# One string of single-engine steps for attention, seams and FFN, with accumulating transfers for part of the third factors

## The chip, the cores and the metric

The kernel runs on one core of a Trainium2 chip. Its engines are TensorE (PE, matrix products into PSUM), VectorE (DVE), ScalarE (ACT), GpSimd (POOL) and SyncE (SP, which here issues transfers); each works through its own queue in order, and they wait for each other through semaphores. The metric is the time of one execution on the device in microseconds (us). Most executions of one kernel agree within 0.3%.

## What is computed

The reference is an attention block with learned inducing points, followed by a gated feed-forward network (FFN) on every token. Four batches of 12416 tokens with 128 channels, 32 inducing vectors, an FFN width of 1536:

```python
def mab(q, kv):
    s = scale * (q @ kv.transpose(0, 2, 1))
    s = s - s.max(-1, keepdims=True)
    a = np.exp(s)
    a /= a.sum(-1, keepdims=True) + 1e-09
    return a @ kv
h = mab(I, x)                       # (4, 32, 128)
x = mab(x, h)                       # (4, 12416, 128)
rms = np.sqrt(np.mean(x * x, axis=-1, keepdims=True) + 1e-06)
xn = x / rms * rms_g
g = xn @ w_gate
silu = g * (1.0 / (1.0 + np.exp(-g)))
val = xn @ w_val
return (silu * val @ w_out)
```

## The kernel before

**Blocks.** A batch is cut into 25 units of 512, 480 or 256 tokens, and the FFN width into 12 columns of 128. A block (b, u, j) is batch, unit and column; there are 1200. For each, `slot` issues the gate product (L743), the silu on ACT (L751), the value product (L754) and the product of silu and value on DVE (L760), which is the factor u of the block. Gate and value products are in float32r, one step of the PE array per column; the attention output is carried as an upper and a lower half, so that these products have both halves in one contraction.

**The output product, in two ways.** For 381 blocks, "plain", the factor goes through one float32 product with `wo` (L676), which the PE array takes in four steps. For the other 819 it is split into an upper and a lower part, and three float32r products take the place of one float32 product: upper part by upper weights and lower part by lower weights into a PSUM bank `u` (L700, L702), and the third, a combination of both parts by a combination of both weights, into `acc` (L676). The combination of the parts is called the third factor below. It is made in `three`:

- kind "sums" (619 blocks): the factor stays in its PSUM bank (the product L760 writes `gv` over itself), ACT makes the upper part (L725), DVE the lower from the upper part in SBUF and the factor in PSUM (L726);
- kind "differences" (200 blocks): the factor is written to an SBUF tile `u`, ACT makes the upper part (L729), POOL the lower (L730), ACT scales the upper (L734);
- in both, one slot later, POOL makes the third factor from both parts with a two-input instruction into a tile of its own (L735).

A set of three tiles (upper, lower, third) is taken from four sets in `xn` buffers and two lent from the `sg` and `sv` weight buffers while they are free; this is why L735 and L726 appear in the profile with the tiles `xn`, `sg` and `sv`.

**Order.** `slots` runs over blocks. Within a slot, the string `ordered` says at which points how many output products of either kind go to PE; `banks` says which of the five PSUM banks each product gets, `holders` which SBUF tile a factor gets; `places` says in which slot each step of the attention of the next batch and each step of a seam stands. A seam (`seam`) turns attention weights into the next unit's normalised operand: transposes and products on DVE, a product on PE (L523), a power on POOL (L539), a multiplication on POOL (L543), a lower half on POOL (L556). Steps may hold instructions of several engines (a score product and its DVE transpose, for instance). The first 47 us, before the first gate product, are written out by hand in `first`.

**Transfers.** All are issued by SP, except three on ACT's queue; POOL issues none.

Of the kernel before, what the change touches and what calls it, by code (L numbers as in the profile page):

```python
# [18 lines left out]
P = 128  # L19
R = 4  # L20
# [3 lines left out]
def kernel(  # L24
# [75 lines left out]
    RING, RESERVE, HELD, SILU = 4, 7, 9, 3  # L100
    LENT = (RING, RING + 1)
# [41 lines left out]
    def load_channels(b, s, k):  # L143

        w = R * per[s]
        if not k:
            xT[b, s] = xtp.tile([P, w * m], F32, name=f"xT{s}")
        nc.sync.dma_start(out=xT[b, s][ts(k, m), :].rearrange("p (w c) -> p w c", c=m),
                          in_=xrows[ds(b * N + start[s], P * per[s]), ts(k, m)].rearrange("(i w) c -> i w c", i=m))
# [159 lines left out]
    def attention(b, load_next):  # L309
# [34 lines left out]
        def scores1(s):  # L344
            nc.vector.tensor_scalar(out=sc[b][:, cols1[s]], in0=scores(s, indT[:], R, per[s]), scalar1=1.0, scalar2=None,
                                    op0=ALU.mult, op1=ALU.max, accum_out=st["gmx"][:, s:s + 1])
# [31 lines left out]
        def sum_h(*sets):  # L378
# [12 lines left out]
            if b and sets[0]:  # L391
                nc.vector.tensor_tensor(out=hl[:, 0:C], in0=hl[:, 0:C], in1=ps[:, 0:C], op=ALU.add)
            elif b:
                nc.scalar.copy(out=hl[:, 0:C], in_=ps[:, 0:C])

        def fold_l():

            nc.vector.reduce_sum(out=st["hl"][:, C:C + 1], in_=st["ls"][:, 0:st["n"]], axis=AX.X)
            ps = bank()
            nc.tensor.matmul(ps[:, 0:1], fold[:].rearrange("p q m -> p (q m)"), st["hl"][:, C:C + 1], start=True, stop=True)  # L400
            rl = st["rl"] = small.tile([P, 1], F32, name="rl")
            nc.vector.reciprocal(out=rl[:], in_=ps[:, 0:1])
# [8 lines left out]
        def turn_h():  # L411

            ps = bank()
            nc.tensor.matmul(ps[:, 0:P], st["hn"], fold[:].rearrange("p q m -> p (q m)"), start=True, stop=True)
            hT = st["hT"] = once.tile([P, P], F32, name="hT")
            if b:
                nc.scalar.copy(out=hT[:], in_=ps[:, 0:P])
                hg = st["hg"] = once.tile([P, P], F32, name="hg")
                nc.scalar.activation(hg[:], ps[:, 0:P], AF.Copy, scale=gam)
            else:  # L420
                nc.vector.tensor_copy(out=hT[:], in_=ps[:, 0:P])
# [5 lines left out]
        def square_h():  # L427
# [4 lines left out]
            ps = bank()  # L432
            nc.tensor.matmul(ps[:, 0:m], st["hT"][:], st["hT"][:, 0:m], start=True, stop=True)
            for q in range(R):
                to, of_ = gram[b][ts(q, m), ts(q, m)], ps[ts(q, m), 0:m]
                nc.scalar.activation(to, of_, AF.Copy, bias=1e-6, scale=1.0 / C)

        def scores2(s):
            ps = scores(s, st["hT"][:, 0:m], quarters[s], per2[s])
            nc.vector.transpose(out=sc[b][rows2[s], cols2[s]], in_=ps)  # L440

        def row_max(s):
            mx = st["mx2"] = small.tile([P, 16], F32, name="mx2")[rows2[s], 0:per2[s]]
            nc.vector.reduce_max(out=mx, in_=weights(b, s), axis=AX.X)

        def sub_max(s):
            n, v, mx = per2[s], weights(b, s), st["mx2"]
# [16 lines left out]
        def stack(i):  # L464


            ps = bank()
            for c, w in enumerate(st.pop(("w", i))):
                nc.tensor.matmul(ps[ts(c, m), :], st["hg"][:, 0:m], w, start=True, stop=True)
            hi, lo = st["halves", i] = [worker([P, 512], F32R, n) for n in ("whi", "wlo")]  # L470
            rows = slice(0, NC * m)
            nc.scalar.copy(out=hi[rows, :], in_=ps[rows, :])
            nc.vector.tensor_tensor(out=lo[rows, :], in0=ps[rows, :], in1=hi[rows, :].bitcast(F32), op=ALU.subtract)
# [33 lines left out]
    def seam(b, s):  # L507
# [41 lines left out]
        def split():  # L549
# [4 lines left out]
            else:  # L554
                nc.vector.tensor_copy(out=hi[rows, 0:w], in_=aT[rows, 0:w])
            engine.tensor_tensor(out=lo[rows, 0:w], in0=aT[rows, 0:w], in1=hi[rows, 0:w].bitcast(F32), op=ALU.subtract)  # L556

        return [turn_a, square, times, scale, root, apply, turn_b, split]
# [11 lines left out]
    plain, kara, waiting = [], [], []  # L570

    def soon(k, step):

        waiting.append([k, step])

    def wait():

        for one in waiting:
            one[0] -= 1
        while any(not one[0] for one in waiting):  # L580
            one = next(one for one in waiting if not one[0])
            waiting.remove(one)
            one[1]()

    def give(group):

        for kind in group:
            (plain if kind == "p" else kara).pop(0)()

    def split_wo(step):  # L590

        if not step:
            kws["first"] = xnp.tile([P, half + NK, C], F32R, name=f"xn{full - 1}")
            rings = [xnp.tile([P, RING, 512], F32R, name=f"xn{full - 4 + n}") for n in range(3)]
            kws["sets"] = [[ring[:, n, :] for ring in rings] for n in range(RING)]
            idle.extend(range(RING))
# [10 lines left out]
        for g in range(2):  # L607
# [8 lines left out]
            if at == 4:  # L616
                nc.gpsimd.tensor_tensor(out=part(2, g)[0], in0=part(1, g)[1], in1=part(0, g)[1], op=ALU.subtract)
            if at == 6:
                scaled(0, g, 4096.0)

    idle, leaving = [], []

    def lend(b, k, idle, leaving):

        if k == (20 if not b else 2):
            idle += LENT
            return True
        if b + 1 < B and k == 184:
            leaving += [n for n in LENT if n not in idle]
            idle[:] = [n for n in idle if n not in LENT]  # L630
        assert k != 192 or not leaving

    def give_back(n, idle, leaving):

        leaving.remove(n) if n in leaving else idle.append(n)

    def lend_tiles():

        tiles = [stk.tile([P, F], F32R, name=name) for name in ("sg", "sv")]
        kws["sets"][RING:] = [[t[:, ts(n, 512)] for n in range(3)] for t in tiles]  # L640

    def split_last(step):

        n = NJ - NK
        if not step:
            kws["last"] = xtp.tile([P, 3 * n, C], F32R, name="xT0")
        one, (whi, wlo, ws) = wo[:, NK:NJ, :], (kws["last"][:, ts(kind, n), :] for kind in range(3))
        if step == 0:
            nc.scalar.activation(whi, one, AF.Copy, scale=1.0 - 2.0 ** -13)
            nc.gpsimd.tensor_tensor(out=wlo, in0=one, in1=whi.bitcast(F32), op=ALU.subtract)  # L650
        if step == 1:
            nc.scalar.activation(wlo, wlo.bitcast(F32), AF.Copy, scale=4096.0)
            nc.gpsimd.tensor_tensor(out=ws, in0=wlo.bitcast(F32), in1=whi.bitcast(F32), op=ALU.subtract)
        if step == 2:
            nc.scalar.activation(whi, whi.bitcast(F32), AF.Copy, scale=4096.0)

    def weight_of(kind, j):
        if j >= NK:
            return kws["last"][:, kind * (NJ - NK) + j - NK, :]
# [3 lines left out]
    def ffn(b, u):  # L663

        s, q = units[u]
        T = per2[s] * m
        a = moving.pop((b, u))
        sg, sv = stacks[b]
        acc = ps_acc.tile([P, 512], F32, name="acc")
        nk = sum((b, u, j) in kinds for j in range(NJ))  # L670
        st = {"left": NJ, "k": nk}
        if nk:
            st["o"] = None

        def project(lhsT, rhs, to):
            nc.tensor.matmul(to, lhsT, rhs, start=st["left"] == NJ, stop=st["left"] == 1)  # L676
            st["left"] -= 1
            if not st["left"]:
                soon(1, finish)

        def finish():
            o = st["o"] if nk else outp.tile([P, 512], F32, name="o")
            whole = o[:, 0:T].rearrange("p (q n) -> p q n", q=R)
            if nk:
                nc.vector.tensor_tensor(out=whole, in0=in_order(acc[:, 0:T]), in1=whole, op=ALU.add)
            else:
                nc.vector.tensor_copy(out=whole, in_=in_order(acc[:, 0:T]))

            def turn():
                nc.vector.transpose(out=o[:, 0:T], in_=o[:, 0:T])  # L690
                soon(2, lambda: store(o))

            soon(1, turn)

        def project3(j, where):
            if st["k"] == nk:
                st["u"] = ps_u.tile([P, 512], F32, name="u3")
            ups = st["u"]
            hi, lo, d = (one[:, 0:T] for one in kws["sets"][where])
            nc.tensor.matmul(ups[:, 0:T], weight_of(0, j), halves_in_turn(hi), start=st["k"] == nk, stop=False)  # L700
            st["k"] -= 1
            nc.tensor.matmul(ups[:, 0:T], weight_of(1, j), halves_in_turn(lo), start=False, stop=not st["k"])  # L702
            if not st["k"]:
                o = st["o"] = outp.tile([P, 512], F32, name="o")
                nc.scalar.activation(o[:, 0:T].rearrange("p (q n) -> p q n", q=R), in_order(ups[:, 0:T]), AF.Copy,  # L705
                                     scale=1.0 + 2.0 ** -12)
# [609 lines left out]
```

## Time and profile before

| what | value |
|---|---|
| time, three runs | 1538.06 us median (1537.92 to 1538.15) |
| profiled execution | 1538.19 us, span 1536.4 us |
| PE | 1518.3 us busy, 99% of the span |
| DVE | 1442.3 us, 94% |
| POOL | 1418.5 us, 92% |
| ACT | 1292.2 us, 84% |
| transfers by SP | 36.2% of 16 DMA engines' span |
| granted PE clock | 1.0 in every slice |

The profile's span is the time from the first to the last instruction of one profiled execution; 1.8 us of the measured time lie outside it. Busy shares are the union of an engine's instructions. A matmul is shown with a length of about 380 ns, but the next begins about 213 ns later, so a PE that is "busy" may still have small waits in it. A group line gives the source line, engine, operation, tiles, shapes and count, then the busy time in us and the mean length in ns, then the idle time before it and what ended that. In the timeline the columns are start in us, length in us, engine, line, operation and tiles.

### The profile page before, as it was taken

How to read it: one execution, taken by the hardware profiler on the slowest of the kernel's cores; microseconds unless marked ns; L12 is line 12 of the kernel's file. 1: busy time of each engine (PE TensorE's matmuls, PEld its weight loads, DVE VectorE, ACT ScalarE, POOL GpSimd, SP SyncE). 2: the span in 40 equal slices, each digit the busy share in tenths (PEclk: the TensorE clock that was granted, in tenths of full speed). 3: DMA queues.
4: the chain of work that ended last, by engine and by line, in shares of the span. 5: the costliest groups of instructions: out<-in, count | busy, mean ns of one | idle time of the engine just before them, and what ended most of it. 6: DMA issues, size and time to landing. Idle time of an engine off the chain costs nothing.

```text
span 1536.4 us, 26105 instructions
## 1 busy us (share of the span) xinstructions
PE 1518.3 (99%) x7141; PEld 1091.8 (71%) x7141; DVE 1442.3 (94%) x2519; ACT 1292.2 (84%) x2501; POOL 1418.5 (92%) x1158
## 2 busy tenths in 40 slices
PE   8999999999999999999999999999999999999998
PEld 6556667767776667776777667676677777777776
DVE  6999999999999998999999999899999999999997
ACT  5777889888888889887988888978798888888886
POOL 1379999999999999999999999899989999999997
PEclk9999999999999999999999999999999999999999
DMA  7345535435453242634444323353222222122221
GB/s 282 91 81 94 97 60 114 90 78 91 67 92 69 38 93 37 137 84 86 72 78 82 56 59 77 74 120 75 49 39 39 38 36 37 34 40 38 40 40 28
DMA packets 389331, 112.58 MB, mean 73 GB/s; under 512 B 365088, under 2 KB 369728, under 8 KB 386624
## 3 DMA queue, kind: packets, MB, share of 16 engines
q1 hardware_dynamic: 388592, 110.83, 36.2%
q8 instruction: 57, 0.93, 0.3%
q14 instruction: 90, 0.74, 0.2%
q10 hardware_dynamic: 592, 0.08, 0.0%
HBM read 53.95 MB, written 27.00 MB: 53 GB/s over the span
## 4 chain that ended last, share of the span: by engine, by line
PE 90%; DVE 3%; POOL 3%; ACT 2%; issue 1%; DMA 0%; DVEq 0%; POOLq 0%; ACTq 0%
PE acc L676 30%; PE gv L743 17%; PE gv L754 16%; PE u L700 10%; PE u L702 10%; PE gv L341 3%; PE gv L523 1%; PE gv L390 1%; POOL xn L735 1%; ACT silu L751 1%; PE gv L820 1%; DVE u L760 1%; POOL xn L730 0%; DVE gv L760 0%; DMA xn<-in_x_dram 0%
## 5 line engine op out<-in xcount | busy, mean ns | idle before, releaser
L735 POOL TENSOR_TENSOR xn<-xn,xn 128x512 fp32r<-128x512 f32 (+2 forms) x626 | 767.6, 1248 | 34.1 <-DVE xn L726 11.6
L751 ACT ACTIVATE silu<-gv 128x512 f32<-128x512 f32 (+2 forms) x1186 | 683.4, 588 | 98.4 <-PE gv L743 88.1
L754 PE MATMUL gv<-a,sv 128*128 128x512 f32 (+2 forms) x1188 | 551.2, 465 | 1.0 <-ACT silu L751 0.4
L743 PE MATMUL gv<-a,sg 128*128 128x512 f32 (+2 forms) x1188 | 472.2, 398 | 1.6 <-ACT silu L751 0.6
L760 DVE TENSOR_TENSOR gv<-silu,gv 128x512 f32<-128x512 f32 (+2 forms) x616 | 410.6, 673 | 23.4 <-PE gv L754 7.5
L760 DVE TENSOR_TENSOR u<-silu,gv 128x512 f32<-128x512 f32 (+2 forms) x570 | 369.4, 655 | 24.4 <-ACT silu L751 8.8
L676 PE MATMUL acc<-u,wo 128*128 128x512 f32 (+2 forms) x762 | 371.2, 577 | 0.0
L725 ACT ACTIVATE xn<-gv 128x512 fp32r<-128x512 f32 (+2 forms) x472 | 278.1, 589 | 62.3 <-DVE gv L760 47.2
L726 DVE SCALAR_TENSOR_TENSOR xn<-xn,gv 128x512 fp32r<-128x512 f32 (+2 forms) x472 | 312.5, 662 | 13.1 <-ACT xn L725 7.4
L743 PEld LDWEIGHTS gv<-a,sg 128*128 128x128 f32 x1188 | 224.1, 189 | 137.4 <-issue 26.7
L754 PEld LDWEIGHTS gv<-a,sv 128*128 128x128 f32 x1188 | 224.3, 189 | 116.5 <-ACT silu L751 34.4
L700 PE MATMUL u<-xn,xn 128*128 128x512 f32 (+2 forms) x599 | 233.7, 390 | 0.0
L676 PE MATMUL acc<-xn,more 128*128 128x512 f32 (+2 forms) x599 | 225.7, 377 | 1.4 <-POOL xn L735 1.2
L730 POOL TENSOR_TENSOR xn<-u,xn 128x512 fp32r<-128x512 f32 (+2 forms) x154 | 191.0, 1240 | 5.1 <-ACT xn L729 4.7
L676 PEld LDWEIGHTS acc<-u,wo 128*128 128x128 f32 x762 | 142.9, 190 | 32.2 <-issue 15.4
L700 PEld LDWEIGHTS u<-xn,xn 128*128 128x128 f32 x599 | 113.3, 189 | 25.6 <-ACT o L705 8.0
L676 PEld LDWEIGHTS acc<-xn,more 128*128 128x128 f32 x599 | 113.1, 189 | 24.4 <-POOL xn L735 10.2
L735 POOL TENSOR_TENSOR sg<-sg 128x512 fp32r<-128x512 f32 (+2 forms) x97 | 123.4, 1272 | 3.6 <-DVE sg L726 1.0
L735 POOL TENSOR_TENSOR sv<-sv 128x512 fp32r<-128x512 f32 (+1 forms) x96 | 122.1, 1272 | 1.6 <-DVE xT L324 0.2
L702 PE MATMUL u<-xn,more 128*128 128x512 f32 (+2 forms) x304 | 113.0, 372 | 0.0
L702 PE MATMUL u<-xn,xn 128*128 128x512 f32 (+2 forms) x295 | 109.8, 372 | 0.0
L729 ACT ACTIVATE xn<-u 128x512 fp32r<-128x512 f32 (+2 forms) x154 | 95.3, 619 | 14.2 <-DVE u L760 9.2
(229 smaller groups left out, 1894.7 us busy)
## 6 DMA issues: line engine op xcount, KB each, us to landing
out_dram<-o SPq DMA_DIRECT2D x320, 64.0 KB, 2.0
xT<-in_x_dram SPq DMA_DIRECT2D x60, 256.0 KB, 3.9
xn<-in_x_dram SPq DMA_DIRECT2D x60, 256.0 KB, 5.0
a<-hi SPq DMA_DIRECT2D x156, 64.0 KB, 2.0
a<-lo SPq DMA_DIRECT2D x156, 64.0 KB, 2.0
xn<-in_x_dram SPq DMA_DIRECT2D x5, 1024.0 KB, 9.7
xn<-w SPq DMA_DIRECT2D x18, 256.0 KB, 3.0
out_dram<-o SPq DMA_DIRECT2D x64, 60.0 KB, 2.0
```

The costliest lines, as they stand in the source:

```text
L676: nc.tensor.matmul(to, lhsT, rhs, start=st["left"] == NJ, stop=st["left"] == 1)
L700: nc.tensor.matmul(ups[:, 0:T], weight_of(0, j), halves_in_turn(hi), start=st["k"] == nk, stop=False)
L702: nc.tensor.matmul(ups[:, 0:T], weight_of(1, j), halves_in_turn(lo), start=False, stop=not st["k"])
L725: nc.scalar.activation(hi, v, AF.Copy, scale=(1.0 - 2.0 ** -13) * 2.0 ** -12)
L726: nc.vector.scalar_tensor_tensor(out=lo, in0=hi.bitcast(F32), scalar=-4096.0, in1=v, op0=ALU.mult, op1=ALU.add)
L729: nc.scalar.activation(d, v, AF.Copy, scale=1.0 - 2.0 ** -13)
L730: nc.gpsimd.tensor_tensor(out=lo, in0=v, in1=d.bitcast(F32), op=ALU.subtract)
L735: nc.gpsimd.tensor_tensor(out=d, in0=hi.bitcast(F32), in1=lo.bitcast(F32), op=ALU.subtract)
L743: nc.tensor.matmul(g[:, 0:T], sg[:, ts(j, P)], halves_in_turn(a[:, 0:T]), start=True, stop=True)
L751: nc.scalar.activation(sl[:, 0:T], g[:, 0:T], AF.Silu)
L754: nc.tensor.matmul(v[:, 0:T], sv[:, ts(j, P)], halves_in_turn(a[:, 0:T]), start=True, stop=True)
L760: nc.vector.tensor_tensor(out=t[:, 0:T], in0=sl[:, 0:T], in1=v[:, 0:T], op=ALU.mult)
```

## The change

Everything after the first 26 blocks is issued from one string, `program`, of 10,709 letters, each one instruction (or one pair) on one engine; a dot stands for an attention or seam step, listed in `taken`, and those steps are cut so that each has instructions of one engine. `slot`, `three`, `soon`, `wait`, `give` and the lending of weight tiles go away. New letter strings give the banks, workers and tiles. The numbers of gate, value and factor products stay.

Blocks now have seven kinds. P is plain (352 blocks with the first 26). S, T and D are split: S with the factor in PSUM (S and s, 328 blocks), T with the factor in an SBUF tile but the lower part still on DVE (T and t, 307 blocks), D with the factor in SBUF and the lower part on POOL (D and d, 213 blocks). The third factor is written over the lower part, after PE has read it: for a capital letter by POOL's two-input instruction (450 blocks), for a small letter by a transfer that POOL issues and that adds the upper part to the lower part in SBUF (398 blocks). The tiles for factors and parts come from one ring of 19. The core of the diff:

```diff
-        def three(j, t):
-            where = idle.pop(0)
-            hi, lo, d = (one[:, 0:T] for one in kws["sets"][where])
-            v, kind = t[:, 0:T], kinds[b, u, j]
-            if kind == "sums":
-                nc.scalar.activation(hi, v, AF.Copy, scale=(1.0 - 2.0 ** -13) * 2.0 ** -12)
-                nc.vector.scalar_tensor_tensor(out=lo, in0=hi.bitcast(F32), scalar=-4096.0, in1=v,
-                                               op0=ALU.mult, op1=ALU.add)
-            else:
-                nc.scalar.activation(d, v, AF.Copy, scale=1.0 - 2.0 ** -13)
-                nc.gpsimd.tensor_tensor(out=lo, in0=v, in1=d.bitcast(F32), op=ALU.subtract)
-            def rest():
-                if kind != "sums":
-                    nc.scalar.activation(hi, d.bitcast(F32), AF.Copy, scale=2.0 ** -12)
-                nc.gpsimd.tensor_tensor(out=d, in0=hi.bitcast(F32), in1=lo.bitcast(F32), op=ALU.subtract)
-                kara.append(lambda: project3(j, where))
...
+    def times_value():
+        n, b, u, j = next_of("m")
...
+        if kind in "Ss":
+            factor_of[n] = {"u": v[:, 0:T]}
+        else:
+            factor_of[n] = {"u": factor()[:, 0:T]}
...
+    def high():
...
+        hi = t["hi"] = room()[:, 0:T]
+        t["lo"] = room()[:, 0:T]
+        if kind in "Dd":
+            nc.scalar.activation(hi, t["u"], AF.Copy, scale=1.0 - 2.0 ** -13)
+        else:
+            nc.scalar.activation(hi, t["u"], AF.Copy, scale=-(1.0 - 2.0 ** -13) * 2.0 ** -12)
...
+    def low():
+        nc.vector.scalar_tensor_tensor(out=t["lo"], in0=t["hi"].bitcast(F32), scalar=4096.0, in1=t["u"],
+                                       op0=ALU.mult, op1=ALU.add)
+    def low_of_u():
+        nc.gpsimd.tensor_tensor(out=t["lo"], in0=t["u"], in1=t["hi"].bitcast(F32), op=ALU.subtract)
+    def high_down():
+        nc.scalar.activation(t["hi"], t["hi"].bitcast(F32), AF.Copy, scale=-(2.0 ** -12))
+    def project_two():
...
+        nc.tensor.matmul(ups, weight_of(0, j), halves_in_turn(t["hi"]), start=not one["q"], stop=False)
+        nc.tensor.matmul(ups, weight_of(1, j), halves_in_turn(t["lo"]), start=False, stop=last)
+        lists["D" if kinds[n].islower() else "d"].append(n)
...
+    def add_in_place():
+        nc.gpsimd.tensor_tensor(out=t["lo"], in0=t["hi"].bitcast(F32), in1=t["lo"].bitcast(F32), op=ALU.add)
+    def add_by_transfer():
+        nc.gpsimd.dma_start(out=t["lo"].bitcast(F32), in_=t["hi"].bitcast(F32), accum_op=ALU.add)
+    def project_third(name):
+        n = lists[name].pop(0)
+        project(n, weight_of(2, blocks[n][2]), halves_in_turn(factor_of[n]["lo"]), False)
...
-    for b in range(B):
-        unit, at = {}, placed(b)
-        for k, (u, j) in slots(b):
-            groups = picks.pop(0)
...
+    do = {"g": gate, "s": silu, "y": lambda: silu(True), "x": gate_times, "v": value, "m": times_value, "h": high, "l": low,
+          "n": low_of_u, "e": high_down, "q": project_two, "d": add_in_place, "D": add_by_transfer,
+          "r": lambda: project_third("r"), "R": lambda: project_third("R"), "p": project_plain, "E": take_upper, "F": finish,
+          "T": turn_out, "O": store, "a": lambda: gather(*next(gathered))}
+    for name in "".join(program.split()):
+        if name == ".":
+            step, args = micros[int(next(taken))]
+            step(*args)
+        else:
+            do[name]()
```

## The prediction

> **What bounds the kernel now.** First the page's busy shares, then the windows (columns: PE, PEld, DVE, ACT, POOL busy us and counts, PE clock, DMA share, GB/s):
>
> ```profile
> PE 1518.3 (99%) x7141; PEld 1091.8 (71%) x7141; DVE 1442.3 (94%) x2519; ACT 1292.2 (84%) x2501; POOL 1418.5 (92%) x1158
> ```
>
> ```profile
> 400.00:600.00 200.00, 199.57 (x855) 144.13 (x854) 192.79 (x343) 172.25 (x341) 194.91 (x160) 1.00 0.37 67
> 1200.00:1400.00 200.00, 199.07 (x800) 147.09 (x798) 193.61 (x320) 173.08 (x329) 195.71 (x153) 1.00 0.20 37
> ```
>
> PE sets the pace, but DVE and POOL stand at 96 to 98% in these stretches: there is room in none of the three. PE's true work is a little less than its busy share. In the chain two plain products take 1.72 us, so one takes 0.86, and float32r products begin 0.213 us apart. With a mean width of 497 of 512 columns (0.97): 2400 gate and value products and 3 x 819 split ones, 4857 x 0.213 x 0.97 = 1003 us; 381 plain ones, 318; the chain's shares for scores (L341, 3%), seams (L523, 1.5%) and sums (L390, 1.1%), 86. That is 1407. With 47 us before the first gate product and some 8 at the end, about 74 of the 1536 us are PE waiting inside the stream.
>
> **The groups that the change touches**, by form:
>
> ```profile
> L735 POOL TENSOR_TENSOR xn<-xn,xn 128x512 fp32r<-128x512 f32 x487 | 615.1, 1285 | 28.0 <-DVE xn L726 8.5 <-PE acc L676 6.2 <-PE gv L754 2.2
> L726 DVE SCALAR_TENSOR_TENSOR xn<-xn,gv 128x512 fp32r<-128x512 f32 x370 | 250.7, 677 | 8.8 <-ACT xn L725 4.3
> L735 POOL TENSOR_TENSOR xn<-xn,xn 128x480 fp32r<-128x480 f32 x112 | 133.2, 1211 | 5.1 <-DVE xn L726 3.1
> ```
>
> A POOL two-input instruction adds 615.1 / 487 = 1.263 us at 512 wide, 1.19 at 480 and 0.72 at 256. L726 adds 0.68 us on DVE; it reads one operand from SBUF (`xn`) and one from PSUM (`gv`). That second operand is the point of this prediction.
>
> **DVE and POOL in each other's way.** Before, very few DVE instructions read two SBUF operands. They are in the timeline, beside POOL:
>
> ```profile
> 317.38 3.77 POOL L735 TENSOR_TENSOR xn<-xn,xn 128x512 fp32r<-128x512 f32 x3
> ...
> 320.55 1.16 DVE L448 TENSOR_TENSOR sc<-sc,mx 128x512 f32<-128x512 f32 x1
> ...
> 321.12 1.73 POOL L730 TENSOR_TENSOR xn<-u,xn 128x512 fp32r<-128x512 f32 x1
> ```
>
> ```profile
> 49.02 1.26 POOL L287 TENSOR_TENSOR xn<-o,we 128x512 f32<-128x512 f32 x1 [4.90 <-PE gv L743]
> ...
> 49.52 1.31 DVE L279 SCALAR_TENSOR_TENSOR we<-sv,we 128x512 int32<-128x512 int32 x1
> ```
>
> ```profile
> L350 DVE TENSOR_TENSOR owns<-gmx,quarter x3: 180/1242/1260, 218.4 to 962.3; 128x28 f32<-128x28 f32 x3
> ```
>
> L448 normally takes 0.68. Here it starts 0.6 us before POOL's third instruction ends (317.38 + 3.77 = 321.15) and takes 1.16; the POOL instruction after it takes 1.73 and not 1.29. L279 starts in the middle of a POOL instruction and takes 1.31 where its median is 0.68; it is the kind of instruction (scalar, tensor, tensor) that makes the lower part. L350 handles 28 columns: 0.18 us alone, 1.24 and 1.26 when it meets a POOL instruction that has just begun. So a DVE instruction with two SBUF operands waits until POOL's running two-input instruction has ended, and the reverse. L726 and L760, with one operand in PSUM, show nothing of this.
>
> **The change, part by part.**
>
> *PE.* 29 plain products become split ones: 20 at 512, 7 at 480, 2 at 256, each 0.86 - 3 x 0.213 = 0.22 us at 512. Gain 6 us.
>
> *ACT.* Upper parts 848 + 213 scalings against 819 + 200, 42 more x 0.6 = 25 us. ACT goes from 1292 to 1317, 84 to 86%: hidden, by its own slack of over 200 us; without that it would be 25 us at most.
>
> *DVE, without waiting.* Lower parts 635 against 619, and 7 more blocks whose silu is a tanh with one more DVE instruction (L748): 23 x 0.61 (instructions overlap by some 0.07) = 14 us. DVE 1456.
>
> *DVE, waiting.* In the 307 T blocks the lower part reads the upper part and the factor, both in SBUF. How often POOL is inside a two-input instruction: by widths there are 526, 108 and 29 of them (450 thirds, 213 lower parts), 664 + 129 + 21 = 814 us, and 81 us from seams and maxima; 895 of some 1600 us, 0.56. Met at a random point, half of 1.26 is left: 0.56 x 0.63 = 0.35 us each, 108 us in all. Ends: the six steady instructions above (three L350, three L448) waited 1.06, 0, 1.08, 0.48, 0 and 0, mean 0.44 at a POOL share of 0.91, so 0.27 at 0.56, 83 us; if POOL's instructions bunch and its share is 0.66, 0.42, 129 us. I take 108, the middle and the direct computation. Nothing hides it: DVE had 94 us idle in all, 26 of it before 120 us and after 1500.
>
> The Trainium skill ("SBUF — State Buffer", SBUF: two separate sides) says that such a pair locks the shared port for the whole instruction, whichever started first; by it POOL's power (L539, 2.9 us) would lock too. But the 0.18 us L350, at 591.8, ran inside a power instruction, so the measurement decides against it here; by the page the sum would be some 20 us more.
>
> *POOL.* Two-input instructions 828, 152 and 39 by width before, 526, 108 and 29 after: 302 x 1.263 + 44 x 1.19 + 10 x 0.72 = 440 us less. 398 issues come in. No POOL issue is in this trace. The bounds are SP's, about 0.62 us (four in 2.49 us at 317.47), and the longest instruction POOL has, L539's 2.9. I take 0.95, between SP's and a two-input instruction's 1.26, nearer to the rows of ordinary work. Waits on DVE: about half of the 307 are followed at once by a POOL instruction that waits some 0.4 us, 63 us. POOL: 1418 - 440 + 378 + 63 = 1419, as busy as before.
>
> *New waits.* The third factor is written over the lower part, so POOL's instruction or issue waits for PE's two products; behind it in POOL's queue stand lower parts, powers and other issues. Between POOL's instruction and PE's third product there are 6 product steps on average (1.3 us, just the length of the instruction), so a POOL instruction that is late is a PE wait. For transfers it is 18 steps, 3.8 us, 5% of them under 2.6.
>
> ```profile
> xn<-in_x_dram SPq DMA_DIRECT2D x60, 256.0 KB, 5.0
> w<-xn SPq DMA_DIRECT2D x4, 256.0 KB, 2.2
> xn<-w SPq DMA_DIRECT2D x18, 256.0 KB, 3.0
> ```
>
> Plain transfers of this size land in 2.2 to 5.0 us. Up to 3.0 they are covered; at 5.0 PE would wait 1.2 us for each, 480 us. I take 3.0, the row of long runs like these, so nothing. The skill ("DMA: Bandwidth & Descriptors", Anatomy of one DMA) gives 2.0 us plus bytes by 436 thousand per us for POOL's path, an estimate of 2.6 us, and would also hide it.
>
> *The moved steps.* Attention, seam and SP instructions are the same in number and length (1081 on SP in both built programs, 1200 gate products and so on); only their places in the queues change. That is worth at most PE's 74 us of waits, and can cost as much where an order without slack is disturbed; I take nothing, since DVE's sum above is what ends last.
>
> **The sum.** DVE becomes the bound: 1456 + 108 = 1564 busy, the 26 us at both ends, and of the 68 us that it idled in between about half, 35, since PE no longer holds it up: span 1625, measured 1627. With order in the queues made without slack for POOL's lateness I take 1630. Low end 1456 + 83 + 26 = 1565; high end 1456 + 129 + 26 + 68 = 1679. PE's 6 us are lost in its own new idle time.
>
> **Rivals.**
>
> 1. *The new order wins (0.25).* One step per instruction lets PE run without some of its 74 us of waits. That decides if T's waiting is short: DVE reaches 1534 only if 307 waits cost under 52 us, 0.17 each, with no idle between. That needs POOL's share at T's lower parts to be 0.27, not 0.56: they would fall into issues and gaps. For it: 398 thirds are no longer POOL instructions that DVE can meet. Against: 663 still are. Time: 1538 - 6 - 15 of waits = 1517, between 1495 and 1534.
>
> 2. *POOL's issues or the transfers' landing decide (0.12).* POOL has 118 us idle before, 80 of it unavoidable at the ends; its span is 978 + 63 + 80 + 398c, and passes 1630 at c = 1.28 us per issue. At 2.0 the time is 1917. Landing at 4.3 us costs 0.5 x 398 = 200 us of PE waits, less its slack: about 1690 to 1740.
>
> 3. *It doesn't tell (0.03).* Gains and waits cancel within 0.2% (about 3 us, what a measurement of this kernel can tell from none).
>
> The change does what it says: 398 accumulating issues stand in POOL's queue of the built program, 450 additions in place, 307 lower parts with two SBUF operands.
>
> **How the numbers follow.** DVE bound by waits, 0.60, 1567 to 1681, likeliest 1630. Slower in all: 0.60 + 0.12 = 0.72. Faster 0.25, same 0.03. The range leaves out 0.08 below (the best third of rival 1, under 1510) and 0.10 above (most of rival 2, over 1705): 1510 to 1705. The likeliest case's own range is 1567 to 1681.
>
> **What would show it.** In the profile after: the lower-part instruction (L743) with tiles `xn` or `u` on both sides at a mean near 1.0 us with many at 1.2 and over, beside 0.68 for those that read `gv`; POOL two-input instructions with a tail at 1.6 and 1.7; DVE busy near 1565 us and above PE's need; PE waiting on DVE and POOL. Wrong: both kinds of L743 at 0.68; POOL queue time of an issue well over 1.3 us; PE waiting mostly on landings.

## The result and the profile after

The changed kernel takes 1809.62 us (median of 4 runs, 1804.33 to 1816.22), against 1538.09 for the kernel before in the same session: a ratio of 1.1768, 95% interval 1.1726 to 1.1809, or 271 us. The profiled execution has a span of 1805.6 us. The forecast was 1630, with 1705 as its upper end: the direction was right, the size was not.

First the busy shares and the two windows that were shown for the kernel before (same columns).

```profile
PE 1615.4 (89%) x7170; PEld 1116.9 (62%) x7170; DVE 1643.3 (91%) x2542; ACT 1321.4 (73%) x2543; POOL 1363.7 (76%) x1200
```

```profile
400.00:600.00 200.00, 186.05 (x763) 131.59 (x761) 192.34 (x305) 158.60 (x313) 168.91 (x154) 0.97 0.72 120
1200.00:1400.00 200.00, 179.49 (x772) 123.06 (x771) 180.50 (x274) 144.30 (x281) 156.80 (x135) 0.96 0.54 102
```

DVE now has more busy time than any other engine, as forecast. But in the second window no engine is near 200: PE 179, DVE 181, POOL 157. So a chain of waits runs through them, and not one full engine. The granted clock is 0.96 to 0.97, where it was 1.00 (0.968 over the whole run). DVE's sum closes the account: 1643 busy and 162 idle make the span, where the forecast had 1564 and 61.

The groups by form, in order: POOL's additions, the issues of the accumulating transfers, the lower parts with two SBUF operands (T), and one with a PSUM operand.

```profile
L789 POOL TENSOR_TENSOR xn<-xn,xn 128x512 fp32r<-128x512 f32 x136 | 206.3, 1527 | 31.1 <-PE u L770 21.5 <-ACT silu L692 3.6 <-DVE gv L724 2.4
...
L795 POOL DMA_DIRECT2D xn<-xn x207 | 204.4, 999 | 127.7 <-PE u L770 33.0 <-PE gv L682 25.8 <-PE gv L710 25.6
...
L743 DVE SCALAR_TENSOR_TENSOR xn<-xn,u 128x512 fp32r<-128x512 f32 x134 | 185.3, 1386 | 5.6 <-PE acc L781 3.5 <-ACT xn L737 1.7 <-issue 0.4
...
L743 DVE SCALAR_TENSOR_TENSOR u<-xn,u 128x512 fp32r<-128x512 f32 x121 | 147.7, 1221 | 1.4 <-ACT xn L737 1.1
...
L743 DVE SCALAR_TENSOR_TENSOR xn<-xn,gv 128x512 fp32r<-128x512 f32 x123 | 82.6, 673 | 0.3 <-ACT xn L737 0.2
```

The one instruction, L743, takes 0.67 us with an operand in PSUM, and 1.22 to 1.39 with both in SBUF. Taken over all 307 T blocks and against 0.675, 0.64 and 0.41 us by width, the waits sum to 188 us, 0.61 each.

The third view is the list of DMA issues (KB each, median us from issue to landing), and the waits of PE and its weight loads (us in all, times, longest).

```profile
xn<-xn POOLq DMA_DIRECT2D x176, 256.0 KB, 4.0
u<-xn POOLq DMA_DIRECT2D x164, 256.0 KB, 4.3
...
a<-lo SPq DMA_DIRECT2D x156, 64.0 KB, 3.0
```

```profile
PEld acc L781 <- DMA xn<-xn: 60.1, 57, 6.8
...
PEld acc L781 <- DMA u<-xn: 54.6, 53, 6.0
...
PE acc L781 <- DMA xn<-xn: 36.5, 27, 6.5
...
PE acc L781 <- DMA u<-xn: 31.9, 30, 5.2
```

```profile
DMA to landing us min/median/max: 2.6/4.1/12.7
```

PE's third products do wait for landings, up to 6.8 us at a time. The last line, from the view of the issuing line L795, gives the reason: the median is 4.1 us, but the slowest landing took 12.7; one in ten took 6.3 or more. PE's weight loads waited for 110 of the 398.

Two suspects stand in these views: the T lower part's second SBUF operand, and the transfers.

### The profile page after: what moved, and what is told of

Same layout as the page of the kernel before. It is cut to its first block, busy times and chain, and to the rows that moved or that the text cites. A ratio compares the mean times of both kernels' runs of the same rounds, so it can differ in the third digit from the quotient of the medians.

```text
span 1805.6 us, 26319 instructions
## 1 busy us (share of the span) xinstructions
PE 1615.4 (89%) x7170; PEld 1116.9 (62%) x7170; DVE 1643.3 (91%) x2542; ACT 1321.4 (73%) x2543; POOL 1363.7 (76%) x1200
## 5 line engine op out<-in xcount | busy, mean ns | idle before, releaser
L724 DVE TENSOR_TENSOR u<-silu,gv 128x512 f32<-128x512 f32 (+2 forms) x855 | 549.4, 658 | 69.7 <-PE gv L710 57.2
L789 POOL TENSOR_TENSOR u<-xn,u 128x512 fp32r<-128x512 f32 (+2 forms) x226 | 325.4, 1463 | 67.0 <-PE u L770 58.6
L795 POOL DMA_DIRECT2D xn<-xn x207 | 204.4, 999 | 127.7 <-PE u L770 33.0
L789 POOL TENSOR_TENSOR xn<-xn,xn 128x512 fp32r<-128x512 f32 (+2 forms) x177 | 259.6, 1480 | 32.9 <-PE u L770 23.2
L795 POOL DMA_DIRECT2D u<-xn x190 | 192.9, 1043 | 63.4 <-PE u L770 13.1
L724 DVE TENSOR_TENSOR gv<-silu,gv 128x512 f32<-128x512 f32 (+1 forms) x324 | 213.6, 667 | 27.4 <-PE gv L710 25.9
L743 DVE SCALAR_TENSOR_TENSOR xn<-xn,u 128x512 fp32r<-128x512 f32 (+2 forms) x157 | 207.8, 1327 | 5.7 <-PE acc L781 3.5
L743 DVE SCALAR_TENSOR_TENSOR u<-xn,u 128x512 fp32r<-128x512 f32 (+2 forms) x148 | 180.5, 1220 | 4.3 <-ACT xn L737 3.9
L781 PE MATMUL acc<-u,more 128*128 128x512 f32 (+2 forms) x345 | 163.2, 479 | 23.5 <-DMA u<-xn 22.5
L750 POOL TENSOR_TENSOR u<-u,xn 128x512 fp32r<-128x512 f32 (+2 forms) x108 | 158.2, 1469 | 19.7 <-ACT xn L734 14.4
```

The costliest lines, as they stand in the source:

```text
L724: nc.vector.tensor_tensor(out=to, in0=sl[:, 0:T], in1=v[:, 0:T], op=ALU.mult)
L743: nc.vector.scalar_tensor_tensor(out=t["lo"], in0=t["hi"].bitcast(F32), scalar=4096.0, in1=t["u"], op0=ALU.mult, op1=ALU.add)
L750: nc.gpsimd.tensor_tensor(out=t["lo"], in0=t["u"], in1=t["hi"].bitcast(F32), op=ALU.subtract)
L781: nc.tensor.matmul(to.rearrange("p (n h) -> p h n", h=2) if step2 else to, lhsT, rhs, start=one["left"] == NJ, stop=one["left"] == 1)
L789: nc.gpsimd.tensor_tensor(out=t["lo"], in0=t["hi"].bitcast(F32), in1=t["lo"].bitcast(F32), op=ALU.add)
L795: nc.gpsimd.dma_start(out=t["lo"].bitcast(F32), in_=t["hi"].bitcast(F32), accum_op=ALU.add)
```

## The experiments

Each kernel is the changed kernel with the edit shown, unless said otherwise. Each time is a median beside the kernel before (1538.06 to 1538.55 in all sessions), with the ratio and its 95% interval. The edits are shown shortened; `...` marks what is left out.

### Both waits, alone and together

**One operand.** The T lower part reads the upper factor alone.

```
-nc.vector.scalar_tensor_tensor(out=t["lo"], in0=hi, scalar=4096.0, in1=t["u"], ...)
+nc.vector.tensor_scalar(out=t["lo"], in0=hi, scalar1=1.0, ..., accum_out=part[:])   # T blocks
```

> The lower part of the 307 T blocks is made by a DVE instruction that reads only the upper part from SBUF (so its value is another; everything else stands as in the changed kernel). It adds one accumulator read of 0.08 us each, 25 us on DVE. Theory A (DVE starves behind POOL at instructions with two SBUF operands): the T lower parts fall from 1.27 us to about 0.68, POOL's two-input instructions from 1.53 to 1.29, and some 170 us of the 270 lost come back: 1610 to 1660. Theory B (PE waits for the landing of the transfers, 4.0 to 4.3 us against a lead of 3.8): the lower parts get shorter, but PE waits on landings as before, 1740 or more.

Measured: 1666.52 us, ratio 1.0834 (1.0818 to 1.0850). The lower parts fall to 0.67 us, and 143 us go, although the edit itself adds 307 accumulator reads of 0.08 us on DVE.

```profile
L745 DVE TENSOR_SCALAR_CACHE_REDUCE xn<-xn 128x512 fp32r<-128x512 f32 x134 | 89.9, 674 | 11.1 <-PE acc L786 8.4 <-ACT xn L737 1.3 <-PE gv L682 1.2
```

POOL's two-input records had been expected to fall to 1.29 us. They stay at 1.56 to 1.58, so it is not DVE that lengthens them.

**No wait for the landing.** PE's third product after a transfer reads the upper factor.

```
-project(n, ..., halves_in_turn(factor_of[n]["lo"]), False)
+project(n, ..., halves_in_turn(factor_of[n]["hi" if name == "R" else "lo"]), False)
```

> The third product of the 398 transfer blocks reads the upper part instead of the tile that the transfer writes (another value), so PE no longer waits for a landing; the transfers still run and still hold their tile. Theory A (lock): at most 100 us come back, 1710 to 1790, T lower parts stay at about 1.27 us. Theory B (landing): PE's waits on DMA, some 180 us by the list of waits, vanish and with them most of the loss: 1580 to 1650.

Measured: 1784.91 us, 1.1611 (1.1574 to 1.1648): 25 us less.

**Both edits together.**

> Both edits together. If lock and landing are the whole loss, the string runs about as its order is meant to: 1490 to 1550. If POOL's issue time (1.0 us each) or the in-place waits matter by themselves, it stays above 1600.

Measured: 1607.77 us, 1.0452 (1.0433 to 1.0472). Without the second operand, the landing wait is worth 59 us (1667 to 1608) and not 25: the two waits cover each other. But 69 us over the kernel before remained, against the first expectation, and became the next question.

**POOL additions in the transfers' place.**

```
-nc.gpsimd.dma_start(out=lo, in_=hi, accum_op=ALU.add)
+nc.gpsimd.tensor_tensor(out=lo, in0=hi, in1=lo, op=ALU.add)
```

> All 398 transfers become POOL's two-input additions in place; the result stays the same. POOL gets 398 x (1.27 - 1.0) = 107 us more, and its share of two-input instructions rises from about 0.55 to 0.8. Theory A: DVE's T lower parts starve longer, mean over 1.6 us, and the time rises over 1850. Theory B: no landing to wait for, so the time falls to 1650 to 1750.

Measured: 1743.77 us, 1.1344 (1.1295 to 1.1394), 66 us *less* than with the transfers, though the transfers were there to relieve POOL. This variant leaves nothing out, and the time is theory B's. POOL is busy 1570 us (90%), so T lower parts meet it more often; they take 1.22 to 1.39 us in the mean (512 and 480 columns), not over 1.6, and their waits sum to 182 us.

### Is the rest the new order, or the transfers?

**One operand, and POOL additions** (the first and the fourth edit together).

> The changed kernel with both: the T lower part reads one SBUF operand only (it leaves out the lower part's value in the T blocks), and the 398 transfers are POOL additions in place. No pair of SBUF operands on DVE, no transfer. Theory A, the rest that stayed after both waits were taken away (1608 against 1538) is the price of the transfers beside POOL (its two-input instructions at 1.59 instead of 1.29 us, tiles that come free late): without transfers POOL's instructions go back to 1.28 to 1.32 and the time to 1530 to 1580. Rival B, the new string itself, with steps written in place and no slack, is the slower order: 1600 to 1640, though POOL's instructions are short.

Measured: 1617.03 us, 1.0512 (1.0496 to 1.0528). The number fits the rival, and POOL's instructions are short again (1.29 us). POOL is busy 1461 us and PE's third products wait for it, so it is the string together with 398 more POOL additions that is slow; the next run takes these away.

```profile
PEld acc L786 <- POOL xn L794: 79.8, 135, 1.6
PEld acc L786 <- POOL u L794: 67.2, 121, 1.8
```

**No addition at all**, on top of the first two edits.

```
-nc.gpsimd.dma_start(out=lo, in_=hi, accum_op=ALU.add)
```

> The changed kernel with the one-operand T lower part and with no transfer at all: 398 third factors are left out, and PE's third product reads the upper factor. It leaves out the T lower part's value and 398 additions. Theory A (transfers carry the rest): POOL falls to about 930 us, its instructions to 1.28, PE waits for nothing but the start, 1490 to 1530, so 80 to 115 less than with transfers whose landing nobody waits for (1608). Rival B (the string itself): 1570 to 1610, PE waiting on DVE or ACT.

Measured: 1508.79 us, 0.9809 (0.9795 to 0.9824). With 398 third factors neither made nor waited for, the string is 29 us *faster* than the kernel before.

```profile
PE 1490.0 (99%) x7170; PEld 1104.9 (73%) x7170; DVE 1439.4 (95%) x2849; ACT 1301.3 (86%) x2543; POOL 988.5 (66%) x802
```

This is rival 1's mechanism (1517), PE running without some of its waits. But the run does less work than the kernel before, which makes all its third factors on POOL in 1538 us; the new string with all of them on POOL and one operand took 1617. So what the order gains when they are made is not shown.

**The two operands, without any transfer** (the same, with the T lower part as changed).

> The changed kernel with its two-operand T lower part but no transfer at all (398 additions are left out, PE's third product reads the upper factor). Theory A, each T lower part is passed over by POOL instructions that follow each other without a gap; without 398 issues POOL has more gaps: the lower part falls from 1.32 to 0.9 to 1.1 us, the time to 1560 to 1640. Rival B, the wait is set by how often a two-input instruction runs, and 663 of them still do: the lower part stays at 1.2 to 1.35 us, 1660 to 1720.

Measured: 1577.80 us, 1.0259 (1.0241 to 1.0276), 69 us over the run before it.

```profile
L743 DVE SCALAR_TENSOR_TENSOR xn<-xn,u 128x512 fp32r<-128x512 f32 x134 | 137.4, 1029 | 1.7 <-ACT xn L737 1.6
...
L743 DVE SCALAR_TENSOR_TENSOR u<-xn,u 128x512 fp32r<-128x512 f32 x121 | 109.9, 909 | 1.9 <-ACT xn L737 1.7
```

The waits sum to 86 us, 0.28 each. That lies at the low end of what the prediction's step gave (83 to 129, 108 taken). It is also theory A's number (0.9 to 1.1 us, 1560 to 1640), but not its reason: where no gap follows, DVE is hardly ever passed here (counts below). With transfers the same edit costs 143 (1667 to 1810) or 177 (1608 to 1785).

**The two operands in the kernel before.** Every other lower part of the sums blocks in a unit, 333 of 619 in all; their values are left out.

```
-in1=v
+in1=hi.bitcast(F32) if len(odd) % 2 else v
```

> The kernel before, with one edit: every other lower part of the sums blocks (310 of them) reads the upper part twice, two SBUF operands, and not the PSUM bank (it leaves out their value). POOL stands at 92% here. Theory A, a waiting DVE instruction is passed over until POOL has a gap, and here gaps are rare: those lower parts take 1.6 us or more, the time is 1700 to 1850. Rival B, it gets in when POOL's running instruction ends: 0.56 to 0.6 us of waiting, 1.25 us each, 310 x 0.58 = 180 us less the 68 us that DVE idled: 1640 to 1670.

Measured: 1688.09 us, 1.0975 (1.0958 to 1.0991).

```profile
L729 DVE SCALAR_TENSOR_TENSOR xn<-xn 128x512 fp32r<-128x512 f32 x193 | 230.3, 1193 | 5.9 <-ACT xn L727 2.6
```

These lower parts take 1.19 us: a wait of 0.52, close to rival B's 0.56 to 0.6; theory A had 1.6 us and over for the whole instruction. The time is 18 us above rival B's range, which had counted 310 of them. So in a full POOL queue a waiting DVE instruction is seldom passed.

### What of a transfer costs?

All of these have one operand and no landing wait (1608 with full transfers, 1509 with none), except where said.

**A POOL stand-in of the issue's length.** An addition over five eighths of the columns; it measures 0.87 us.

```
-nc.gpsimd.dma_start(out=lo, in_=hi, accum_op=ALU.add)
+nc.gpsimd.tensor_tensor(out=lo[:, 0:w], in0=hi[:, 0:w], in1=lo[:, 0:w], op=ALU.add)   # w = T * 5 // 8
```

> The kernel without both waits (the T lower part has one SBUF operand, PE's third product after a transfer reads the upper factor: 1608), and with a POOL addition over five eighths of the columns, an estimated 0.85 us, in the place of each of the 398 transfers: what POOL's queue takes for an issue when it is full (0.85 us from end to end). No transfer at all. It leaves out the T lower part's value and the 398 third factors. Without transfers and stand-ins the string takes 1509. Theory A, POOL's time for issues, which makes its other results late, is the rest: 1570 to 1610. Rival B, the transfers in flight (two tiles held for 4 to 5 us, gathers at 3.0 us and not 2.0) are the rest: 1510 to 1540.

Measured: 1508.95 us, 0.9811 (0.9795 to 0.9827). POOL is busy 320 us more than without, and the time does not move: POOL's time for issues costs nothing in this kernel, where no result of theirs is waited for.

**Transfers of a sixteenth of the bytes.**

```
-nc.gpsimd.dma_start(out=lo, in_=hi, accum_op=ALU.add)
+nc.gpsimd.dma_start(out=lo[:, 0:32], in_=hi[:, 0:32], accum_op=ALU.add)
```

> The same kernel without both waits, with all 398 transfers issued, but each of 32 columns and not 512: a sixteenth of the bytes, the same 128 rows. It leaves out the T lower part's value and most of 398 third factors. Theory A, issues on POOL are the rest: they stay near 1.0 us, and the time at 1580 to 1610. Rival B, the transfers' bytes and landing: landing falls from 4.4 to about 2.5 us, gathers back to 2.0, and the time to 1515 to 1550.

Measured: 1575.73 us, 1.0242 (1.0227 to 1.0258), between the two expectations. The median landing falls to 2.6 us, but the longest is still 10.1.

**The same small transfers with the two-operand lower part.**

> The changed kernel with its two-operand T lower parts, the same small transfers of 32 columns, and PE's third product after them reading the upper factor. It leaves out most of 398 third factors. Theory A, POOL's instructions begin before the one before them has ended because an issue went ahead of them, whatever it moves, and then pass the waiting DVE instruction: the T lower parts stay at 1.25 to 1.35 us, 1730 to 1790. Rival B, it is the bytes in flight: 0.95 to 1.05 us as without transfers, 1580 to 1640.

Measured: 1750.51 us, 1.1378 (1.1347 to 1.1409). T lower parts stay at 1.26 to 1.32 us: the long waits do not need the bytes.

**Issues that hold no factor tile**, small ones first; the full ones move 512 columns of a weight tile.

```
-nc.gpsimd.dma_start(out=lo[:, 0:32], in_=hi[:, 0:32], accum_op=ALU.add)
+nc.gpsimd.dma_start(out=spare[k // 16][:, ts(k % 16, 32)], in_=ident[:, 0:32])
```

> The kernel without both waits, with 398 issues on POOL of 128 rows of 32 columns as before, but from a constant tile to spare memory (not accumulating), so that no factor tile waits for a landing. It leaves out the T lower part's value and the 398 third factors. The same issues with factor tiles held until landing took 1576, a POOL stand-in without transfers 1509. Theory A, a factor tile that comes back to the ring only when its transfer has landed (up to 10 us after its issue) is what stays of the transfers' price: 1509 to 1525. Rival B, the issues themselves disturb POOL or DVE, whatever they move: 1560 to 1580.

> The same, but each transfer moves 128 rows of 512 columns (256 KB) from a weight tile to spare memory: the full bytes beside the gathers and loads, and still no factor tile held. The full transfers that hold factor tiles took 1608. Theory A, holding is nearly all of the price: 1509 to 1535, though gathers land at 2.5 to 3.0 us and not 2.0. Rival B, the load on the DMA queues, which makes gathers late for PE: 1560 to 1600.

Measured: 1517.85 us, 0.9865 (0.9850 to 0.9880), and with 256 KB each 1519.99, 0.9887 (0.9871 to 0.9904). For plain transfers that hold nothing, the full bytes add 2 us. That does not clear the bytes of accumulating ones: these keep the DMA engines busy twice as long for the same data, here first the kernel with both edits (1608) and then the plain full ones.

```profile
q0 software_dynamic: 57312, 102.28, 36.9%
...
q0 software_dynamic: 31840, 104.36, 18.2%
```

The columns are packets, MB and the share of 16 engines' span. The chain of the full, accumulating, holding transfers shows where time goes: DMA carries 7% of it (some 113 us; the transfers' own landings are 5 of the 7), against 2% in the two runs that hold nothing. In the view of the holding kernel's issuing line, the ones that wait for a landing are no longer PE, but those who want the tile next (the longest of 35 waits, 81 us in all):

```profile
who waited for it (us, times):
  ACT xn L734: 17.2, 9
  DVE xn L748: 16.2, 6
  ACT xn L737: 14.3, 6
  POOL u L755: 13.6, 4
```

But these issues were also plain ones, of 0.56 us. So two runs took holding and accumulating apart, both with 32 columns: the first edit is the held transfer without `accum_op`, the second the transfer to spare memory with it.

```
+nc.gpsimd.dma_start(out=lo[:, 0:32], in_=hi[:, 0:32])
+nc.gpsimd.dma_start(out=spare[k // 16][:, ts(k % 16, 32)], in_=ident[:, 0:32], accum_op=ALU.add)   # the other run
```

> The kernel without both waits, with 398 small transfers (32 columns) from the upper factor to the lower part as in the run of 1576, but plain ones that do not accumulate: factor tiles are held until landing, nothing is added. It leaves out the T lower part's value and the 398 third factors. Theory A, holding the tiles is the price: with landings near 1.9 to 2.6 us it stays at 1555 to 1580. Rival B, accumulating is the price (issues of 1.1 us and not 0.55, POOL's instructions that begin early, late landings): 1515 to 1530.

> 398 small transfers from a constant tile that accumulate onto spare memory, no factor tile held; the plain ones took 1518. It leaves out the T lower part's value and the 398 third factors. Theory A, holding: 1515 to 1530. Rival B, accumulating: 1555 to 1580, with issues near 1.1 us.

Measured: held and plain 1543.19, 1.0038 (1.0022 to 1.0054); accumulating and not held 1527.91, 0.9940 (0.9923 to 0.9958). With small transfers, over 1518 for neither: accumulating costs 10 us, holding 25, both 58. Each theory had expected the whole price on its side. Together they cost more than the sum of the two, 35. A likely reason, not tested apart, is that accumulating makes the landing later (medians 1.9 us plain, 2.6 held and accumulating, 3.1 onto spare memory), and a held tile pays for each late landing. With full bytes the same pair of edits takes 1608, 32 us more than with small ones; full transfers that only hold, or only accumulate, were not run.

**The two operands with small, plain, held transfers.**

> The changed kernel with its two-operand T lower parts and 398 small transfers that hold their tiles but do not accumulate; PE's third product after them reads the upper factor. It leaves out the 398 third factors. The accumulating ones took 1751, with T lower parts at 1.26 to 1.32 us. Theory A, only accumulating issues make POOL's instructions begin before the one before has ended and so pass the waiting DVE instruction: T lower parts at 0.9 to 1.05 us as without transfers, 1600 to 1640. Rival B, any issue in POOL's queue does it: 1.2 to 1.35 us, 1690 to 1740.

Measured: 1682.13 us, 1.0934 (1.0915 to 1.0952), T lower parts at 1.07 to 1.23 us: between the two, so neither theory holds whole.

### Who passes the waiting DVE instruction

One passage of the changed kernel's timeline (start, length, in us; lines of other work left out):

```profile
730.89 1.58 POOL L789 TENSOR_TENSOR xn<-xn,xn 128x512 fp32r<-128x512 f32 x1
...
731.33 5.38 DVE L743 SCALAR_TENSOR_TENSOR u<-xn,u 128x512 fp32r<-128x512 f32 x1
...
732.12 1.57 POOL L750 TENSOR_TENSOR xn<-u,xn 128x512 fp32r<-128x512 f32 x1
...
733.36 2.79 POOL L789 TENSOR_TENSOR u<-xn,u 128x512 fp32r<-128x512 f32 x2
```

L743 comes 0.44 us after a POOL instruction has begun. It is passed by three more and ends at 736.71, when POOL's run is over (736.15). Without transfers it looks so:

```profile
943.47 1.29 POOL L789 TENSOR_TENSOR xn<-xn 128x512 fp32r<-128x512 f32 x1
...
943.50 1.80 DVE L743 SCALAR_TENSOR_TENSOR xn<-xn,u 128x512 fp32r<-128x512 f32 x1
...
944.71 1.72 POOL L789 TENSOR_TENSOR u<-xn,u 128x512 fp32r<-128x512 f32 x1
```

Here DVE gets in when the running instruction ends, and it is the next POOL instruction that waits (1.72). Counted over the traces, where POOL's next two-input instruction follows without a gap, it passes the waiting DVE in 55 of 111 cases in the changed kernel and in 43 of 92 with small plain transfers. Without any issue in POOL's queue the counts are 24 of 253 (POOL additions), 1 of 92 (no third factor) and 9 of 162 (the kernel before with the edit). How overlapping records are counted moves these (POOL additions to 51 of 280 in another count), but not their order. Where an issue or a gap follows, DVE nearly always gets in: 128 of 132 cases in the changed kernel. So passing is several times as frequent with issues among POOL's instructions. It is not their bytes. But issues are not needed for it: with POOL additions in their place, five T lower parts took 4.8 to 6.6 us, each passed by three to five POOL instructions, and 6.6 is the longest of all runs. What decides that the next instruction passes is not shown; accumulating adds to it (188 us of waits against 146, both with small transfers), but is not all of it.

## Why the prediction was wrong, by its own steps

The account, from the runs, each line with something more than the one above (the first four with the one-operand lower part):

| kernel | us |
|---|---|
| the string, 398 third factors left out, one operand | 1509 |
| with 398 plain issues that hold nothing, small / full bytes | 1518 / 1520 |
| with full accumulating transfers that hold their tiles | 1608 |
| with PE waiting for the landing | 1667 |
| with the two-operand T lower part: the changed kernel | 1810 |

**Right.** ACT's and DVE's plain work: ACT 1321 against 1317, and DVE without its waits 1643 - 188 = 1455 against 1456. POOL does not set the end: its busy time is 1364 us, and a stand-in for each issue cost nothing. POOL's share in two-input instructions was 0.57 of the span, where 0.56 was taken. That a power instruction does not make DVE wait, read from one row, holds: 11 T lower parts that began well inside one (L560) took 0.63 to 0.69 us. The issue, put at 0.95 us, measures 1.00 to 1.04 in its record, and about 0.85 from the end of the instruction ahead of it to its own end when the queue is full. The mechanism of the term, two SBUF operands on DVE against POOL, is shown by removal (143 us) and by adding it to the kernel before (150 us).

**"DVE, waiting": 108 us, measured 188.** The step had DVE wait for what is left of the running instruction, and then get in. That holds in the mean where no issue stands in POOL's queue: 0.28 us each without transfers, and 0.52 in the kernel before and 0.59 with POOL additions, where POOL's share in two-input instructions is 0.85 and 0.86 and the same step gives 0.54. In the changed kernel, 39 of the 307 waits are longer than 1.2 us and make 104 of the 188 us: DVE is passed. The end at 129 did not cover it, because it too let DVE in at the end of the running instruction. The six steady instructions of the low end, with a mean wait of 0.44 us before, had 0.25 to 4.7 us each in the changed kernel.

**"I take 3.0 ... so nothing": the transfers cost 158 us** (1509 to 1667, without the second operand). Two steps failed here. A landing was taken as one number, from rows of plain transfers, and compared with a mean lead of 3.8 us; it is a spread of 2.6 to 12.7 us, with a median of 4.1, and the part over the lead is what PE waits for (59 us). And the tiles were left out: both factor tiles of a transfer go back to the ring only after its landing, which no step priced. Holding and accumulating together cost 88 us for full transfers, over the 1520 of plain ones that hold none; how the 88 divide was measured for small ones alone (58, of which holding alone makes 25 and accumulating alone 10). The bytes of plain transfers, with gathers at 2.3 us and not 2.0, add 2 us. With these waits in it, DVE's idle time, put at 61 us, measured 162. The two misses, 80 and 101 us, make the forecast span of 1625 into 1806.

**"The moved steps", taken as nothing.** The string takes 1509 where rival 1's number was 1517, but only with 398 third factors left out. So 29 us is the most that the order is shown to gain.

**Rival 2** had 1690 to 1740 at a landing of 4.3 us; with the lock taken away, 1667 was measured. That is near, but in part by luck: its price was PE's waits alone, which make 59 us, and held tiles were not in it. The mistake was also to hold it against the lock as an alternative, where the two came together. They enlarge each other: 69 us for the lock alone and 158 for the transfers would make 1736, 74 less than measured.

**The longer POOL records** (1.53 us and not 1.28) were foretold as a tail, from waits on DVE. They are there without any such wait (1.56 to 1.63), and they are mostly overlap: after accumulating issues an instruction is recorded as begun some 0.3 us before the one ahead of it has ended (a median), while from end to end POOL's two-input instructions in a run stay 1.23 us apart in the mean (1.31 with the lock).

The Trainium skill ("SBUF — State Buffer", SBUF: two separate sides) says that whichever of such a pair starts first has the shared port for the whole instruction. That agrees with the mean waits in the runs without issues (0.28 and 0.52 us); it does not tell of the several POOL instructions that pass a waiting DVE one here, for up to 5 us. The same section warns that a DVE instruction in a two-port mode keeps POOL from writing a transfer's descriptors. The two-operand lower parts are not why landings are late here: with one operand in the T lower parts they were as late (median 4.3, longest 11.7 us).

## What to carry to other kernels

Price a wait between engines in the queue that the change will make, and not in the one that is there: with issues among POOL's instructions, waits that had been worked out about rightly for a queue without them came out twice as long (0.61 us against 0.28). A transfer in place of an instruction costs its landing twice, once for the reader and once for the tiles that it keeps out of their ring, and in both it is a minority that is waited for (110 waits of PE's weight loads, and 35 for the tiles, at 398 landings), so the spread counts more than the median. When two costs may come together, run the change with each removed and with both removed before calling one of them the cause.

## What was not expected of the hardware

- A DVE instruction with two SBUF operands took up to 5.6 us in the changed kernel instead of 0.68, passed by several POOL instructions that followed each other. Without issues in the queue most got in at the end of the running instruction, but with POOL additions one took 6.6 us.
- An accumulating issue of 128 rows takes some 0.85 us of POOL's queue from end to end, and a plain one 0.51, whether each row moves 128 bytes or 2 KB. Landings grow with the transfers in flight at the issue: in the changed kernel means of 4.0 us with none, 4.4 with one, 5.6 with two and 7.8 with three. What made single small transfers land after 8 to 10 us stays open.
- PE's granted clock was 0.968 in the changed kernel and 0.963 without its landing wait, 0.982 with one operand, 0.993 with POOL's additions, and 0.999 with full plain transfers that hold nothing. In the traces it falls to half in stretches of 3.4 or 6.8 us, and the number of these follows PE's pauses of more than 2 us: until PE's last product there are 25 stretches and 25 such pauses in the changed kernel, 11 and 10 with one operand, 6 and 5 with POOL's additions. The sum of PE's idle time does not decide: the kernel before with two operands has 95 us of it, one pause over 2 us and no such stretch. In the changed kernel the stretches make 112 us at half clock, up to 56 us of PE's time; how much of that is in the 271 us is not shown.
